# Preparing twelve of a layer's sixteen weight tiles inside the attention stage instead of eight, four of them in place

## The chip, the cores and the metric

The kernel runs on one core of one Trainium2 chip. The metric is the device time of one execution in microseconds (us), given as the median of three runs.

## The reference, cut to what matters

Attention with a computed bias (4 batches, 8 heads, 576 positions, 64 per head), then two feed-forward layers of width 2048 over the 2304 tokens. The weights arrive as 64-bit floats.

```python
scores = scale * np.matmul(q, k.transpose(0, 1, 3, 2)) + bias
attn = np.exp(scores - np.max(scores, axis=-1, keepdims=True))
attn = attn / (np.sum(attn, axis=-1, keepdims=True) + 1e-09)
x = np.matmul(attn, v)                    # 2304 tokens x 512
h = x @ moe_w_in;  x = (h * np.cos(h)) @ moe_w_out
h = x @ moe2_w_in
out = (np.maximum(h, 0.0) + alpha * np.minimum(h, 0.0)) @ moe2_w_out
```

## The kernel before

**Attention.** The eight heads are taken two at a time, so there are 16 pairs (head pair, batch), head pairs outermost. A pair has five row blocks: two in its unit A, three in its unit B (a half-size one first). For each block TensorE computes the scores (L339), VectorE adds the bias and takes the row minimum of the negated sum in one pass out of PSUM (L355), ScalarE takes the exponential (L368). Transposes on TensorE (L421, L386, L430, L443), copies out of PSUM on VectorE and ScalarE (L408, L406) and the products with v (L456, L453) follow as "fillers" between later score blocks. The variable `j` of the loop counts 64 rows; it runs from 0 to 144, nine per pair. Units A of the first four pairs come first, then their units B, then the other twelve pairs one after another, from `j` = 36 on.

**Weight tiles.** Each layer has 16 weight tiles `f`; a tile has two halves, part 0 from `w_in` and part 1 from `w_out`, each 128 x 512. `weight` is a generator that prepares one half: SyncE's queue issues the load of the raw 64-bit words (`raw`, two buffers, L168); ScalarE reads the upper and the lower words (L172 into `c`, L173 into `p`, two buffers each); VectorE moves the exponent and the sign into place (L175, L176); GpSimd adds the low bits (L179). The 32-bit result is split into a rounded high part (L187 on GpSimd, L189 on ScalarE) and the rest (L193, GpSimd or VectorE), because TensorE multiplies high and low parts apart. `HIA` and `LOP` say which engine does the two last steps: GpSimd for halves of layer 0 prepared in attention, ScalarE and VectorE for the others. `stage_w` prepares a half in a tile `st` and stores it to DRAM (`w_d`, L200); `fetch_w` brings a whole tile back by a DMA on GpSimd's queue (L208); `direct_w` prepares a half in the place where the layer uses it.

`bg` is the list of such generators; `step(n)` advances it by n yields. In attention a half of layer 0 is added every `WSR` = 6.5 of `j` from `WS0` = 24 on and one step is made per `j`. Tiles 0 to 7 go this way; 0 to 3 are fetched in the last four blocks of attention, 4 to 7 in the first units of the feed-forward stage. Tiles 8 to 15 are prepared in place while layer 0 works on its first token tile, with `QUOTA0` = 9 steps per unit.

**Feed-forward.** There are five token tiles `t` (three of 512, two of 384) and 16 `f` per layer and tile; one (layer, `t`, `f`) is a unit. A unit's 12 matmuls `h` (L622) run four units (`LA`) ahead of its 12 matmuls `o` (L671, L673). Between them stands the activation of layer 0: L631 (ScalarE), L632 and L633 (VectorE), L635 (ScalarE), L636 (VectorE), then the split L654 (ScalarE) and L655 (GpSimd). After a token tile's last `o`, `evac` copies the four sums out of PSUM (L681, L683), and the next token tile's `o` needs these four banks.

**Order.** Each engine takes its instructions in an order fixed when the program is built. A planner lays them out on a simulated timeline by priority, which is program order apart from `high_priority` blocks; it puts an instruction ahead of earlier ones when its inputs and its buffer are there in that simulation. The two last steps of each weight half are kept in program order (`keep`, `KEEP`).

Of the kernel before, what the change touches and what calls it, by code (L numbers as in the profile page):

```python
# [9 lines left out]
F32 = mybir.dt.float32  # L10
F32R = mybir.dt.float32r
# [22 lines left out]
HIA = (2, 1, 1, 1)  # L34
LOP = (1, 0, 0, 0)
EV_A, EV_M = 5, 6
UPB, EPB = {"D": 11, "A": 4}, 4
PBUF, BTB = 6, 10
FIRST, SIDE, SMOD, BFIRST, BRATE, SPL, WS0, WSR, PER = 4, 6, 2, 16, 1.25, 3, 24, 6.5, 1.0
XL, XS, OEB, LA = 7, 12, 3, 4  # L40
KEEP = (1, 1)
QUOTA0, QUOTA1, NSF = 9, 2, 8
ELAG = 1


# [15 lines left out]
def attn_mlp_kernel(ctx: ExitStack, tc: tile.TileContext, a: dict, out: bass.AP):  # L61
    nc = tc.nc
    ve, se, ge, te, sy = nc.vector, nc.scalar, nc.gpsimd, nc.tensor, nc.sync
# [93 lines left out]
    wt = {}  # L157
    wpool = {}
    keep = lambda k, ins: tc.keep_in_program_order(ins) if k < len(KEEP) and KEEP[k] else ins
    wide = a["wi1"].dtype == I64  # L160
    w_d = [dr.tile([NF, 128, 2, 1024], F32, tag=f"w_d{i}", name=f"w_d{i}") for i in range(2)]

    def weight(layer, f, part, hi, lo, hi_act, lo_pool):
        src = (a["wi1"], a["wi2"])[layer][f] if part == 0 else (a["wo1"], a["wo2"])[layer][f * 128:(f + 1) * 128, :]
        nm = f"{layer}_{f}_{part}"
        if wide:
            raw = wpool["s"].tile([128, 512, 2], I32, tag="raw", name=f"raw{nm}")
            sy.dma_start(out=raw.rearrange("p n t -> p (n t)"), in_=src.bitcast(I32))  # L168
            yield
            c = wpool["c"].tile([128, 512], I32, tag="c", name=f"wc{nm}")  # L170
            p = wpool["c"].tile([128, 512], I32, tag="p", name=f"wp{nm}")
            se.activation(out=c.bitcast(F32), in_=raw[:, :, 1].bitcast(F32), func=AF.Copy, scale=2.0 ** -112)  # L172
            se.activation(out=p, in_=raw[:, :, 0].bitcast(U32), func=AF.Copy, scale=2.0 ** -29)  # L173
            yield
            ve.tensor_scalar(c, c, 3, None, op0=ALU.logical_shift_left)  # L175
            ve.scalar_tensor_tensor(out=c, in0=raw[:, :, 1], scalar=-2 ** 31, in1=c,  # L176
                                    op0=ALU.bitwise_and, op1=ALU.bitwise_or)
            yield
            ge.tensor_tensor(out=c, in0=c, in1=p, op=ALU.add)  # L179
            yield  # L180
            w = c.bitcast(F32)
        else:
            w = wpool["s"].tile([128, 512], F32, tag="raw", name=f"raw{nm}")
            sy.dma_start(out=w, in_=src)
            yield
        if hi_act == 2:
            keep(0, ge.tensor_copy(out=hi, in_=w))  # L187
        elif hi_act:
            keep(0, se.activation(out=hi, in_=w, func=AF.Copy))  # L189
        else:  # L190
            keep(0, ve.tensor_copy(out=hi, in_=w))
        yield
        keep(1, (ge if lo_pool else ve).tensor_tensor(out=lo, in0=w, in1=hi.bitcast(F32), op=ALU.subtract))  # L193
        yield

    def stage_w(layer, f, part):
        t = wpool["c"].tile([128, 2, 512], F32R, tag="st", bufs=1, name=f"st{layer}_{f}_{part}")
        yield from weight(layer, f, part, t[:, 0, :], t[:, 1, :], HIA[layer], LOP[layer])
        yield
        sy.dma_start(out=w_d[layer][f, :, :, 512 * part:512 * part + 512], in_=t.bitcast(F32))  # L200
# [6 lines left out]
    def fetch_w(layer, f):  # L207
        ge.dma_start(out=slot(layer, f), in_=w_d[layer][f])  # L208

    def direct_w(layer, f, part):  # L210
        t = slot(layer, f) if part == 0 else wt[layer, f]
        sl = slice(512 * part, 512 * part + 512)
        yield from weight(layer, f, part, t[:, 0, sl], t[:, 1, sl], HIA[layer + 2], LOP[layer + 2])

    bg = []

    def step(n=1):
        for _ in range(n):
            if not bg:
                return  # L220
            g = bg.pop(0)
            try:
                with tc.high_priority(offset=LP):
                    next(g)
            except StopIteration:
                continue
            bg.insert(min(1, len(bg)), g)
# [9 lines left out]
    def attention():  # L237
        with ExitStack() as c:
# [269 lines left out]
            def more_bias(g):  # L508
                nonlocal ng
                while ng < min(g, NG):  # L510
                    next(bias)
                    ng += 1
                    if ng >= SIDE and ng % SMOD == 0:
                        next(side, None)
                    for s, m in GNEED.items():
                        if ng == m:
                            for h in range(2 if s else 1):
                                load_bias(0, s + 4 * h)
                    if ng == NG:
                        for _ in side:  # L520
                            pass
                        bstack.close()
                        for _ in range(2):
                            ps_t.append(c.enter_context(tc.tile_pool(name="ps_8", bufs=1, space=PSUM, reuse_waits="tile")))
                        right = dict(side="right", reuse_waits="tile")
                        wpool["s"] = ctx.enter_context(tc.tile_pool(name="ws", bufs=2, **right))
                        wpool["c"] = ctx.enter_context(tc.tile_pool(name="wc", bufs=2, **right))
                        wpool["a"] = ctx.enter_context(tc.tile_pool(name="wa", bufs=4, **right))

            pend_exp = []  # L530
            fill = []
            waiting = list(units)
            splits = {}
            credit = 0.0
            ns = 0
            NS = len(stages)
            i = j = 0
            while i < NS or pend_exp or waiting or fill:
                new = []
                if i < NS:  # L540
                    n, u, s = stages[i]
                    hp, b = pairs[n]
                    more_bias(max(BFIRST + int(BRATE * j), GNEED[s]))
                    for m in range(FIRST, NP):
                        f = pos[m, 1]
                        if i == f - 6:
                            load_qkv(m)
                            splits[m] = split_qk(m)
                        if f - SPL <= i < f:
                            next(splits[m], None)  # L550
                    while n not in done:
                        next(side, None)
                    pss = emit_S(n, s)
                    new = [(n, s, h) + emit_max(n, s, h, ps) for h, ps in enumerate(pss)]
                for x in range(len(pend_exp) if i >= NS else len(pend_exp) + len(new) - ELAG):
                    if not pend_exp:
                        pend_exp, new = new, []
                    emit_exp(*pend_exp.pop(0))
                pend_exp += new
                if i < NS:  # L560
                    if b == B - 1 and hp + 1 < NHP:
                        for h in range(len(pss)):
                            load_bias(hp + 1, s + 4 * h)
                    if ng == NG and ns < 2 * NSF and j >= WS0 + WSR * ns:
                        bg.append(stage_w(0, ns // 2, ns % 2))
                        ns += 1
                    if i >= NS - 4:
                        fetch_w(0, i - (NS - 4))
                while waiting and all((waiting[0][0], *k) in Pt for k in place if place[k][0] == waiting[0][1]):
                    recip(*waiting[0])  # L570
                    fill += fillers(*waiting.pop(0))
                m = 2 if s else 1
                credit += PER * m
                while fill and (credit > 0 or i >= NS):
                    d, fn = fill.pop(0)
                    credit -= d
                    fn()
                if not fill:
                    credit = min(credit, 0.0)
                step(m)  # L580
                j += m
                i += 1
            step(100)
# [2 lines left out]
    def mlp():  # L586
        with ExitStack() as c:
            xh_p = c.enter_context(tc.tile_pool(name="xh", bufs=8, reuse_waits="tile"))
            g_p = c.enter_context(tc.tile_pool(name="gp", bufs=3, reuse_waits="tile"))
            t_p = c.enter_context(tc.tile_pool(name="tp", bufs=2, reuse_waits="tile"))  # L590
            wpool["b"] = c.enter_context(tc.tile_pool(name="wb", bufs=12, reuse_waits="tile"))
            ph = c.enter_context(tc.tile_pool(name="ph", bufs=4, space=PSUM, reuse_waits="tile"))
            po = c.enter_context(tc.tile_pool(name="po", bufs=4, space=PSUM, reuse_waits="tile"))
# [2 lines left out]
            raw = {}  # L596
# [103 lines left out]
            for j in range(len(units) + LA):  # L700
                quota = 0
                if j < len(units):
                    L, t, f = units[j]
# [8 lines left out]
                    if L == 0 and t == NTI - 1 and f >= 6 and f % 2 == 0 or L == 1 and t == 0 and 2 <= f < 5:  # L712
                        fetch_w(1, nf)
                        nf += 1
                    quota = QUOTA0 if t == 0 else QUOTA1
                    ps = emit_h(L, t, f)
                    acts.append((act1 if L == 0 else act2)(t, f, ps))
                    next(acts[-1])
# [20 lines left out]

    attention()  # L740
    mlp()


# [60 lines left out]
```

## Time and profile before

| | |
|---|---|
| median of three runs | 1181.04 us (1180.21 to 1185.94) |
| the profiled execution, its own time | 1182.64 us |
| its span, first to last instruction | 1180.9 us |
| mean granted TensorE clock | 0.981 |
| TensorE matmul busy | 1127.7 us (96%) |
| VectorE, ScalarE, GpSimd busy | 696.4, 517.2, 437.1 us |

Busy matmul time is not the engine at its peak, since ends of matmuls are modelled. Attention lasts to about 361 us of the span, the feed-forward stage from there. "[2.00 <-DMA raw]" behind an instruction means that its engine stood idle 2.00 us before it, until that event. The engines are called PE (TensorE), PEld (its weight loads), DVE (VectorE), ACT (ScalarE), POOL (GpSimd) and SP (SyncE).

### The profile page before, as it was taken

The numbers are of one execution on the slowest core, as the hardware profiler recorded it, in microseconds if no ns is written. First come the engines' busy times: TensorE is split into PE (matmuls) and PEld (weight loads), VectorE is DVE, ScalarE is ACT, GpSimd is POOL, SyncE is SP. The second block draws the span as 40 slices with busy tenths as digits, with TensorE's granted clock in tenths as the row PEclk, the third lists the DMA queues.
The fourth block names the chain that finished last, engine by engine and source line by source line (L and its number), as shares of the span: only waits on it lengthen the run. The fifth ranks groups of instructions, "written<-read, shape, count | busy, mean of one in ns | idle before, by whom it ended". The sixth has DMA issues, their size and how long they took to land.

```text
span 1180.9 us, 17191 instructions
## 1 busy us (share of the span) xinstructions
PE 1127.7 (96%) x6376; PEld 891.5 (75%) x6376; DVE 696.4 (59%) x1278; ACT 517.2 (44%) x1006; POOL 437.1 (37%) x400
## 2 busy tenths in 40 slices
PE   5698998999998999899999999999999999999998
PEld 1245665666665887788888999988888888889997
DVE  8796566666667987555555556696742332332322
ACT  5586666665665764444443544434411111111111
POOL 5104445445314654333333334454632222322222
PEclk9699999999999999899999999999999999999999
DMA  7657546746316532212212325553310000000000
GB/s 244 199 145 251 186 150 205 235 156 204 104 58 211 206 124 91 78 66 63 90 54 63 108 90 173 192 193 120 106 37 1 27 37 1 27 36 1 27 1 27
DMA packets 56083, 129.47 MB, mean 110 GB/s; under 512 B 8000, under 2 KB 15168, under 8 KB 53952
## 3 DMA queue, kind: packets, MB, share of 16 engines
q1 hardware_dynamic: 53696, 111.60, 29.2%
q0 software_dynamic: 2304, 16.78, 4.1%
q8 instruction: 50, 0.82, 0.3%
q14 instruction: 33, 0.27, 0.1%
HBM read 86.53 MB, written 41.83 MB: 109 GB/s over the span
## 4 chain that ended last, share of the span: by engine, by line
PE 77%; DVE 9%; DMA 5%; ACT 5%; issue 3%; POOL 0%; SPq 0%; DVEq 0%; ACTq 0%; POOLq 0%
PE h L622 29%; PE o L673 17%; PE o L671 14%; PE S L339 5%; PE x_B L456 3%; DVE u L122 2%; PE T_A L421 2%; PE T_B L421 2%; DMA raw<-in_wi_dram 1%; PE x_A L456 1%; DMA raw<-in_wo_dram 1%; PE bps L127 1%; DVE P L355 1%; DMA bias_d<-be 1%; ACT P L368 1%
## 5 line engine op out<-in xcount | busy, mean ns | idle before, releaser
L622 PE MATMUL h<-xhi,w 128*128 128x512 f32 (+1 forms) x1280 | 394.3, 370 | 0.6 <-DVE w L193 0.6
L655 POOL TENSOR_TENSOR glo<-tb,ghi 128x512 fp32r<-128x512 f32 (+1 forms) x160 | 197.4, 1234 | 427.3 <-ACT ghi L654 390.3
L622 PEld LDWEIGHTS h<-xhi,w 128*128 128x128 f32 x1280 | 237.9, 188 | 34.3 <-DVE w L193 1.0
L622 PE MATMUL h<-xlo,w 128*128 128x512 f32 (+1 forms) x640 | 236.5, 370 | 0.0
L654 ACT ACTIVATE ghi<-tb 128x512 fp32r<-128x512 f32 (+1 forms) x160 | 93.1, 583 | 284.2 <-PE o L673 248.7
L671 PE MATMUL o<-ghi,w 128*128 128x512 f32 (+1 forms) x640 | 199.5, 372 | 4.5 <-ACT oe L681 3.4
L673 PE MATMUL o<-w,ghi 128*128 128x512 f32 x576 | 192.1, 392 | 0.0
L644 DVE TENSOR_SCALAR tb<-h,alpha 128x512 f32<-128x512 f32 (+1 forms) x80 | 55.6, 695 | 199.2 <-PE h L622 189.8
L671 PEld LDWEIGHTS o<-ghi,w 128*128 128x128 f32 x640 | 119.7, 189 | 21.4 <-ACT oe L681 3.8
L622 PEld LDWEIGHTS h<-xlo,w 128*128 128x128 f32 x640 | 120.3, 188 | 17.7 <-issue 0.5
L673 PEld LDWEIGHTS o<-w,ghi 128*128 128x128 f32 x576 | 108.2, 188 | 22.7
L179 POOL TENSOR_TENSOR wc<-wc,wp 128x512 int32<-128x512 int32 x64 | 87.7, 1370 | 97.8 <-DVE wc L176 77.8
L671 PE MATMUL o<-glo,w 128*128 128x512 f32 (+1 forms) x320 | 118.7, 371 | 0.7 <-POOL glo L655 0.7
L368 ACT ACTIVATE P<-P,nm 128x576 f32<-128x576 f32 x128 | 98.3, 771 | 45.2 <-DVE nm L355 45.1
L673 PE MATMUL o<-w,glo 128*128 128x512 f32 x288 | 112.9, 392 | 0.0
L355 DVE CUSTOM_DVE_ANT_0 P<-S,bt 128x576 f32<-128x576 f32 x128 | 91.8, 753 | 26.8 <-PE S L339 25.3
L635 ACT ACTIVATE tb<-tb,hpi 128x512 f32<-128x512 f32 (+1 forms) x80 | 54.3, 679 | 101.5 <-DVE tb L633 101.4
L632 DVE SCALAR_TENSOR_TENSOR tb<-ta,h 128x512 f32<-128x512 int32 (+1 forms) x80 | 50.3, 629 | 60.2 <-ACT ta L631 40.2
L636 DVE TENSOR_TENSOR tb<-h,tb 128x512 f32<-128x512 f32 (+1 forms) x80 | 50.8, 635 | 53.8 <-ACT tb L635 53.7
L173 ACT ACTIVATE wp<-raw 128x512 int32<-128x512 uint32 x64 | 42.9, 670 | 62.0 <-DMA raw<-in_wo_dram 32.0
L671 PEld LDWEIGHTS o<-glo,w 128*128 128x128 f32 x320 | 60.7, 190 | 9.1 <-POOL glo L655 1.1
L339 PE MATMUL S<-kh,qh 64*128 64x288 f32 (+1 forms) x288 | 56.7, 349 | 9.2 <-DVE nm L355 9.2
(100 smaller groups left out, 1603.5 us busy)
## 6 DMA issues: line engine op xcount, KB each, us to landing
raw<-in_wi_dram SPq DMA_DIRECT2D x32, 512.0 KB, 3.5
raw<-in_wo_dram SPq DMA_DIRECT2D x32, 512.0 KB, 3.5
w_d<-st SPq DMA_DIRECT2D x32, 512.0 KB, 3.1
w<-w_d POOLq DMA_DIRECT2D x16, 1024.0 KB, 6.7
bias_d<-be SPq DMA_DIRECT2D x36, 295.5 KB, 3.3
xlo<-x_d SPq DMA_DIRECT2D x24, 256.0 KB, 4.3
rq<-in_q_dram SPq DMA_DIRECT2D x16, 320.0 KB, 3.2
rk<-in_k_dram SPq DMA_DIRECT2D x16, 320.0 KB, 3.5
```

What stands on the lines that cost most here:

```text
L179: ge.tensor_tensor(out=c, in0=c, in1=p, op=ALU.add)
L339: te.matmul(ps[:, hf, 0:HS], lhsT=w[r, 128 * i:128 * i + 128], rhs=m[r, c0:c0 + HS], start=(j == 0), stop=(j == 2))
L355: keep(2, ve.tensor_tensor_reduce(out=sn.rearrange("p (a b) -> p a b", a=2), in0=ps[:, :, 0:HS], in1=bt[hp, s].rearrange("p (a b) -> p a b ...
L368: keep(3, se.activation(out=e, in_=e, func=AF.Exp, bias=nm, scale=-1.0, accum_out=sums[n, u][:, col, 0:1]))
L622: te.matmul(ps[:, 0:n], lhsT=w_[:, wx, w], rhs=xx[:, 0:n], start=(j == 0), stop=(j == 11))
L635: se.activation(out=g, in_=g, func=AF.Sin, bias=hpi)
L636: ve.tensor_tensor(out=g, in0=h, in1=g, op=ALU.mult)
L644: ve.tensor_scalar(g, h, 0.0, alpha[:, f:f + 1], op0=ALU.min, op1=ALU.mult)
L654: se.activation(out=ghi[:, 0:n], in_=g, func=AF.Copy)
L655: ge.tensor_tensor(out=glo[:, 0:n], in0=g, in1=ghi[:, 0:n].bitcast(F32), op=ALU.subtract)
L671: te.matmul(acc[L, t][i][:, 0:n], lhsT=w_[:, wx, wl], rhs=gx[:, 0:n], start=st, stop=sp)
L673: te.matmul(acc[L, t][i], lhsT=gx[:, sl], rhs=w_[:, wx, 512:1024], start=st, stop=sp)
```

## The change

Layer 0's halves are added in attention from `j` = 22 on, every 4.6 of `j`, and 1.5 steps are made per `j`. Tiles 0 to 3 (halves 0 to 7) are prepared in place by `direct_w`, with GpSimd for the last two steps as in `stage_w`; tiles 4 to 11 are staged through DRAM as before and fetched in the first eight units of the feed-forward stage. The four fetches at attention's end are gone. Tiles 12 to 15 are left for the first token tile, with 6 steps per unit (layer 1 keeps 9). The load of a half's raw words is written one half ahead of its generator, and `st` has two buffers in attention.

```diff
-FIRST, SIDE, SMOD, BFIRST, BRATE, SPL, WS0, WSR, PER = 4, 6, 2, 16, 1.25, 3, 24, 6.5, 1.0
+FIRST, SIDE, SMOD, BFIRST, BRATE, SPL, WS0, WSR, PER = 4, 6, 2, 16, 1.25, 3, 22, 4.6, 1.0
+SR = 1.5
-QUOTA0, QUOTA1, NSF = 9, 2, 8
+QUOTA0, QUOTA1, NSF = (6, 9), 2, 12
...
+    raws_w = {}
+
+    def load_raw(layer, f, part):
...
+            raw = wpool["s"].tile([128, 512, 2], I32, tag="raw", name=f"raw{nm}")
+            sy.dma_start(out=raw.rearrange("p n t -> p (n t)"), in_=src.bitcast(I32))
...
+        raws_w[layer, f, part] = raw
...
     def weight(layer, f, part, hi, lo, hi_act, lo_pool):
...
-            raw = wpool["s"].tile([128, 512, 2], I32, tag="raw", name=f"raw{nm}")
-            sy.dma_start(out=raw.rearrange("p n t -> p (n t)"), in_=src.bitcast(I32))
-            yield
+            if (layer, f, part) not in raws_w:
+                load_raw(layer, f, part)
+                yield
+            raw = raws_w.pop((layer, f, part))
...
     def stage_w(layer, f, part):
-        t = wpool["c"].tile([128, 2, 512], F32R, tag="st", bufs=1, name=f"st{layer}_{f}_{part}")
+        t = wpool["t"].tile([128, 2, 512], F32R, tag="st", name=f"st{layer}_{f}_{part}")
...
-    def direct_w(layer, f, part):
+    def direct_w(layer, f, part, ahead=0):
...
-        yield from weight(layer, f, part, t[:, 0, sl], t[:, 1, sl], HIA[layer + 2], LOP[layer + 2])
+        i = layer + 2 - 2 * ahead
+        yield from weight(layer, f, part, t[:, 0, sl], t[:, 1, sl], HIA[i], LOP[i])
...
+                        wpool["t"] = c.enter_context(tc.tile_pool(name="wt", bufs=2, **right))
...
                     if ng == NG and ns < 2 * NSF and j >= WS0 + WSR * ns:
-                        bg.append(stage_w(0, ns // 2, ns % 2))
+                        if ns == 0:
+                            load_raw(0, 0, 0)
+                        if ns + 1 < 2 * NSF:
+                            load_raw(0, (ns + 1) // 2, (ns + 1) % 2)
+                        bg.append(direct_w(0, ns // 2, ns % 2, 1) if ns < 8 else stage_w(0, ns // 2, ns % 2))
                         ns += 1
-                    if i >= NS - 4:
-                        fetch_w(0, i - (NS - 4))
...
-                step(m)
+                wsteps += SR * m
+                step(int(wsteps))
+                wsteps -= int(wsteps)
...
+            wpool["t"] = c.enter_context(tc.tile_pool(name="wt", bufs=1, reuse_waits="tile"))
...
-                    quota = QUOTA0 if t == 0 else QUOTA1
+                    quota = QUOTA0[L] if t == 0 else QUOTA1
```

## Rows read from the trace of the kernel before

**Rows 1.** The page's first line.

```profile
span 1180.9 us, 17191 instructions
```

**Rows 2.** Busy time by stretch: PE, PEld, DVE, ACT, POOL, clock, DMA share, GB/s.

```profile
100.00:361.00 261.00, 247.58 (x1997) 166.98 (x1994) 172.88 (x447) 166.66 (x381) 110.89 (x122) 0.99 0.51 165
390.00:450.00 60.00, 59.44 (x261) 48.65 (x260) 56.41 (x73) 42.55 (x72) 36.45 (x26) 1.00 0.44 142
480.80:486.60 5.80, 5.72 (x14) 4.50 (x15) 4.52 (x7) 2.96 (x6) 2.96 (x2) 0.50 0.99 320
```

**Rows 3.** Busy time, weight preparation (tile wc) on VectorE alone, first token tile.

```profile
390.00:450.00 60.00, 35.59 (x41) 1.00 0.44 142
```

**Rows 4.** The same view, the activation (tile tb) on VectorE alone.

```profile
390.00:450.00 60.00, 23.87 (x32) 1.00 0.44 142
```

**Rows 5.** The chain that ended last, one undisturbed unit: start, duration, what.

```profile
502.70 2.73 PE h L622 x12
505.43 2.72 PE o L671 x12
```

**Rows 6.** Timeline to the end of the first token tile: start, duration, instruction.

```profile
445.80 0.72 PE L622 MATMUL h<-xhi,w 128*128 128x512 f32 x2 [0.56 <-DVE w L193]
...
454.86 0.50 PE L671 MATMUL o<-glo,w 128*128 128x512 f32 x1 [0.71 <-POOL glo L655]
...
477.59 1.39 DVE L193 TENSOR_TENSOR st<-wc,st 128x512 fp32r<-128x512 f32 x1 [0.35 <-ACT st L189]
...
479.71 0.43 DVE L175 TENSOR_SCALAR wc<-wc 128x512 int32<-128x512 int32 x1 [0.73 <-ACT wc L172]
480.05 0.68 DVE L683 COPY oe<-o 128x512 f32<-128x512 f32 x1
...
480.88 0.76 PE L671 MATMUL o<-ghi,w 128*128 128x512 f32 x1 [3.44 <-ACT oe L681]
```

**Rows 7.** Groups of instructions in attention, 100 to 361 us, weight preparation only.

```profile
L179 POOL TENSOR_TENSOR wc<-wc,wp 128x512 int32<-128x512 int32 x16 | 20.5, 1278 | 39.2 <-DVE wc L176 19.9 <-DVE sm_A L377 9.6 <-ACT wp L173 5.1
L193 POOL TENSOR_TENSOR st<-wc,st 128x512 fp32r<-128x512 f32 x15 | 19.1, 1276 | 0.2
...
L176 DVE SCALAR_TENSOR_TENSOR wc<-raw,wc 128x512 int32<-128x512 int32 x17 | 12.5, 737 | 0.3
L173 ACT ACTIVATE wp<-raw 128x512 int32<-128x512 uint32 x18 | 12.1, 674 | 14.0 <-DMA raw<-in_wo_dram 7.9 <-DMA raw<-in_wi_dram 3.6 <-POOL ql L326 2.4
L172 ACT ACTIVATE wc<-raw 128x512 f32<-128x512 f32 x17 | 11.2, 661 | 0.8 <-DMA bias_d<-be 0.8
L187 POOL CAST st<-wc 128x512 fp32r<-128x512 f32 x16 | 10.4, 648 | 19.6 <-DMA w_d<-st 19.6
L175 DVE TENSOR_SCALAR wc<-wc 128x512 int32<-128x512 int32 x17 | 7.8, 460 | 11.4 <-ACT wc L172 11.4
```

**Rows 8.** Eleven pairs from first score to first score, with ACT L173 alone.

```profile
193.61:215.48 21.87, 1.31 (x2) 0.92 0.75 236
...
269.64:290.28 20.64, 1.34 (x2) 0.92 0.73 226
...
sum 203.98, ACT 8.06; mean ACT 0.73
```

**Rows 9.** The same eleven pairs, with DVE L176 alone.

```profile
215.48:233.93 18.45, 1.37 (x2) 1.00 0.68 230
...
307.80:326.09 18.29, 1.59 (x2) 1.00 0.38 131
```

**Rows 10.** Timeline inside the first pair of rows 8.

```profile
195.57 0.66 ACT L173 ACTIVATE wp<-raw 128x512 int32<-128x512 uint32 x1 [2.00 <-DMA raw<-in_wo_dram]
...
197.31 0.34 PE L386 MATMUL T_B<-ident,Pr 128*64 128x64 f32 x4 [1.40 <-ACT T_B L406]
...
199.37 0.40 PE L339 MATMUL S<-kh,qh 64*128 64x288 f32 x2 [1.36 <-DVE nm L355]
```

**Rows 11.** The page's DMA issues: KB each, median us to landing.

```profile
w<-w_d POOLq DMA_DIRECT2D x16, 1024.0 KB, 6.7
```

More of the change, by code (lines that the diff above doesn't have):

```diff
@@ L161, in attn_mlp_kernel @@
     w_d = [dr.tile([NF, 128, 2, 1024], F32, tag=f"w_d{i}", name=f"w_d{i}") for i in range(2)]
-    def weight(layer, f, part, hi, lo, hi_act, lo_pool):
+    raws_w = {}
+    def load_raw(layer, f, part):
         src = (a["wi1"], a["wi2"])[layer][f] if part == 0 else (a["wo1"], a["wo2"])[layer][f * 128:(f + 1) * 128, :]
@@ L168, in weight @@
             sy.dma_start(out=raw.rearrange("p n t -> p (n t)"), in_=src.bitcast(I32))
-            yield
+        else:
+            raw = wpool["s"].tile([128, 512], F32, tag="raw", name=f"raw{nm}")
+            sy.dma_start(out=raw, in_=src)
+        raws_w[layer, f, part] = raw
+    def weight(layer, f, part, hi, lo, hi_act, lo_pool):
+        nm = f"{layer}_{f}_{part}"
+        if wide:
+            if (layer, f, part) not in raws_w:
+                load_raw(layer, f, part)
+                yield
+            raw = raws_w.pop((layer, f, part))
             c = wpool["c"].tile([128, 512], I32, tag="c", name=f"wc{nm}")
@@ L182, in weight @@
         else:
-            w = wpool["s"].tile([128, 512], F32, tag="raw", name=f"raw{nm}")
-            sy.dma_start(out=w, in_=src)
-            yield
+            if (layer, f, part) not in raws_w:
+                load_raw(layer, f, part)
+                yield
+            w = raws_w.pop((layer, f, part))
         if hi_act == 2:
@@ L534, in attention @@
             credit = 0.0
+            wsteps = 0.0
             ns = 0
```

## Prediction

> **What bounds the kernel now.** I read the page first, then the busy time by stretch, then the timeline wherever a stretch lost matmuls, then the groups of instructions in attention and the busy time pair by pair. The profiled execution took 1182.64 us, of which 1180.9 lie in the span [rows 1] and 1.7 around it; it is 1.6 above the median of 1181.04. The sum below is made against 1182.64, and what it changes is then taken from the median.
>
> In the feed-forward stage TensorE sets the pace: an undisturbed unit, twelve h and twelve o, takes 2.73 + 2.72 = 5.45 us [rows 5], and no other engine matters as long as it keeps up. The stretch where one does not keep up is layer 0's first token tile. From 390 to 450 us VectorE is busy 56.4 of 60 us [rows 2]. Of that work the weight preparation takes 35.59 us in 41 instructions, three to a half, so 2.60 us per half [rows 3], and the activation 23.87 us in 32, three to a unit, so 2.24 us per unit [rows 4]. (The two overlap a little at their seams, so they add to more than the union.) The reader can check the overload: 9 steps per unit at 7 yields per half are 1.29 halves, and 1.29 x 2.60 + 2.24 = 5.6 us of VectorE in a unit of 5.45. In these 60 us VectorE finished 32 / 3 = 10.7 units' activation where TensorE could do 60 / 5.45 = 11. TensorE hides the lag behind its lead of four units until that is used up. Then it stands 0.56 us for a late weight and 0.71 us for a late activation, and at the end of the token tile 3.44 us for the evacuation [rows 6]: VectorE took the evacuating copy L683 only at 480.05, behind L193 and L175 of layer 1's weights. The clock fell after that stall and was granted at 0.50 (1.2 of 2.4 GHz) for 5.80 us [rows 2], which is worth half of it, 2.9 us.
>
> In attention TensorE shows 247.6 busy us of 261, while VectorE (172.9), ScalarE (166.7) and GpSimd (110.9) have room [rows 2]. Eleven pairs that run one after another take 203.98 us. Two of them stick out, 21.87 and 20.64 us [rows 8]; the other nine average (203.98 - 21.87 - 20.64) / 9 = 17.94. These two are the only ones in which L173, which reads raw words, runs twice. Inside the first, ScalarE stood 2.00 us at the head of its queue for the raw load; the copies and exponentials behind it were late, TensorE stood 1.40 and 1.36 us [rows 10], and the pair's clock mean is 0.92 [rows 8].
>
> **The change part by part.**
>
> *Eight halves leave the first token tile.* VectorE loses 8 x 2.60 = 20.8 us there. The density falls to 6 / 7 = 0.86 halves per unit, so 0.86 x 2.60 + 2.24 = 4.5 us per 5.45: from 103% to 82%, below capacity with 1 us per unit to spare. The lag no longer builds up, and with it go the two small stalls (0.56 + 0.71), the evacuation stall (3.44) and the slow clock behind it (2.9): 7.6 us together. The layer-1 instructions ahead of the evacuation keep their program place, so I bound this from below by the first two alone: 1.3 us.
>
> *Eight halves are added to attention.* One costs ScalarE 661 + 674 ns, VectorE 460 + 737 ns and GpSimd 1278 + 648 + 1276 ns [rows 7]; eight cost 10.7, 9.6 and 25.6 us. All three engines have that room [rows 2], so busy time is not the price; the price is that each instruction stands in order ahead of a score's minimum, an exponential or a copy. Low bound: nothing, since the nine other pairs lie near 17.94 whether they read no raw load or one. High bound: the two held pairs as the price of a second half, (21.87 + 20.64) / 2 - 17.94 = 3.3 us each, x 8 = 26.5. In between lie the two pairs that did the VectorE pass L176 twice without a late load: 18.45 and 18.29 [rows 9], 0.43 above 17.94. I take that row, since it holds the added VectorE work without the accident of a late load: 8 x 0.43 = 3.4 us.
>
> *The steps* must fit: 8 halves x 6 yields + 16 x 7 = 160, and 1.5 x (144 - 22) = 183 are offered, so attention ends with nothing owed. Before, 128 were owed against 120.
>
> *In place and two `st` buffers.* GpSimd's 19.6 us of waiting for the store of `st` [rows 7] should shrink. GpSimd waits on other engines anyway, so I count 0.
>
> *The fetches.* The stores stay sixteen. Four fetches leave attention, and the first token tile has eight instead of four. Each lands 6.7 us after its issue [rows 11]; it is written at unit i for unit i + 4, that is 4 x 5.45 = 21.8 us ahead, so I count 0. Its cover gone, it is a rival below.
>
> *The load half a tile ahead.* With two `raw` buffers a load can go only when the half before the previous one has been read. If the planner already puts loads at that point, writing the load earlier moves nothing; I take 0, with the removal of the held pairs as the other end, -6.6 (3.9 + 2.7).
>
> *Sum:* -7.6 + 3.4 = -4.2 us, 1178.4 for the profiled execution's own time, 1176.8 against the median.
>
> *A rule against the change.* At the stretch of [rows 3] a VectorE preparation instruction averages 35.59 / 41 = 868 ns; in attention the two it has there average (460 + 737) / 2 = 598 [rows 7]. The Trainium skill, page "SBUF — State Buffer", section "Who interferes with whom", says that a VectorE instruction with two SBUF inputs and a GpSimd instruction that reads SBUF shut each other out for a whole instruction; the change puts all its new GpSimd work beside attention's VectorE. By that rule the sum would gain a term (the port rival below); by the 598 ns, measured with sixteen halves beside GpSimd, it does not.
>
> **The rivals.**
>
> *Held pairs (slower).* After the change a half comes every 4.6 of `j` and a pair is nine, so nearly every pair converts two raw loads, and so far both pairs that did were held at 3.3 us. At H held pairs attention changes by 3.3 x (H - 2). It eats the 7.6 from H = 4.3 on and is slower by over 0.5% from six on; with seven, +16.5 - 7.6 = +8.9, 1190. For it: two out of two. Against: pairs next to them had as much VectorE work at 18.4, and the loads were late there, not the work itself.
>
> *Loads early enough.* The load half a tile ahead does remove the held pairs: -4.2 - 6.6 = -10.8, 1170.2. For it: the only large losses in attention start at a raw load. Against: the two buffers.
>
> *The evacuation stall stays,* since layer 1's kept instructions still stand ahead of L683: only 1.3 is won, +2.1, 1183.1.
>
> *Late fetches.* If the eight go strictly one after another, each is 6.7 - 5.45 = 1.25 us later than its unit needs, so up to 10 us late at the eighth: +5.8, 1186.8. Against: four units of lead, and DMA engines that are 0.44 busy in that stretch [rows 2].
>
> *Port.* If GpSimd's new work lengthens the preparation in attention to 868 ns as in [rows 3], 24 halves x 2 x 0.27 = 13 us of VectorE stand ahead of score minima: +8.8 if all is on the path, 1189.8.
>
> **How the numbers follow.** A measurement of this kernel tells about 0.5%, 5.9 us, from no change: 1175.1 to 1186.9. The forecast as summed has 0.42 and its own range is 1173 to 1180 (3.4 between 0 and 7), of which 0.13 falls below 1175.1. Loads early enough 0.21, held pairs 0.16, the stall stays 0.11, late fetches 0.06, port 0.04. Faster: 0.21 + 0.13 = 0.34. Slower: 0.13 of the held pairs (six or more), 0.03 each of the last two: 0.19. Within: 0.47. The range must hold the forecast, the stalls that stay, most of the early loads and some held pairs: 1167 to 1188.
>
> **What would show it.** Right: between 390 and 477 us VectorE at about 80%, no TensorE stall at the end of the first token tile and no clock of 0.50 there, and 24 fewer VectorE preparation instructions in the first token tile (8 x 3). Attention's steps: pairs with two L173 at 18 to 18.5 us (my sum), at 21 (held pairs), or no pair above 18.5 (early loads). SyncE's raw loads still issued as soon as a buffer comes free would show that writing them earlier moved nothing. Wrong: a TensorE wait for a tile fetched by L208, an evacuation copy still behind L193, or attention longer by more than 7.6 us.

## The result and the profile after

The changed kernel takes 1171.3 us (median of 4 runs, 1168.49 to 1173.1), the kernel before 1181.03 beside it (4 runs): a ratio of 0.9915, 95% interval 0.9894 to 0.9936, 0.85% faster. The profiled execution took 1172.02 us with a span of 1170.3. Against the span of before [rows 1] that is 10.6 us less.

The busy time of the changed kernel by stretch has the columns of [rows 2]. The first stretch is attention; the next two are most of layer 0's first token tile, and the last is its end.

```profile
100.00:361.00 261.00, 246.77 (x1999) 167.76 (x1997) 193.79 (x469) 178.19 (x402) 138.12 (x145) 0.99 0.54 173
390.00:450.00 60.00, 60.00 (x265) 49.48 (x264) 43.26 (x57) 32.49 (x54) 28.36 (x24) 1.00 0.51 185
450.00:477.00 27.00, 27.00 (x119) 22.07 (x118) 17.72 (x24) 13.18 (x21) 9.67 (x8) 1.00 0.24 79
477.00:487.00 10.00, 10.00 (x44) 8.10 (x44) 4.14 (x6) 4.07 (x7) 2.54 (x3) 1.00 0.00 0
```

TensorE is busy without a hole through the whole first token tile, where it stood 3.44 us before [rows 6], and the clock stays at 1.00 where 5.80 us ran at 0.50 [rows 2]. VectorE went from 56.41 [rows 2] to 43.26 of 60 us. Its two kinds of work in the same stretch, in the view of [rows 3, 4], first the weight preparation, then the activation:

```profile
390.00:450.00 60.00, 14.65 (x18) 1.00 0.51 185
390.00:450.00 60.00, 27.52 (x35) 1.00 0.51 185
```

There are 23 fewer preparation instructions, and 35 of the activation for 32: VectorE now keeps pace with TensorE's eleven units. The timeline of the changed kernel at the end of the token tile shows VectorE's evacuating copy without an idle time or a queue before it (columns as in [rows 6]):

```profile
467.60 0.43 DVE L190 TENSOR_SCALAR wc<-wc 128x512 int32<-128x512 int32 x1 [0.73 <-ACT wc L187]
467.94 0.68 DVE L707 COPY oe<-o 128x512 f32<-128x512 f32 x1
```

A layer-1 instruction still stands just ahead of it, but VectorE is no longer behind.

The span can be cut at four instructions that the timeline shows: the first score of the fifth pair, the first score of the last pair, the last pair's last score block, and the first h.

| stretch, us | before | after | difference |
|---|---|---|---|
| start to the fifth pair | 140.6 | 144.0 | +3.4 |
| eleven pairs | 204.0 | 202.0 | -2.0 |
| last pair, to its last score block | 15.6 | 13.1 | -2.5 |
| from there to the first h | 7.3 | 5.5 | -1.8 |
| feed-forward, to the end | 813.4 | 805.7 | -7.7 |

The feed-forward stage gained what was forecast for it. Attention gained too, where 3.4 us of loss had been forecast.

### The profile page after: what moved, and what is told of

It reads as the page before. It is cut to its first block, busy times and chain, and to the rows that moved or that the text cites. A ratio compares the mean times of both kernels' runs of the same rounds, so it can differ in the third digit from the quotient of the medians.

```text
span 1170.3 us, 17227 instructions
## 1 busy us (share of the span) xinstructions
PE 1121.2 (96%) x6376; PEld 891.2 (76%) x6376; DVE 694.6 (59%) x1270; ACT 513.1 (44%) x998; POOL 451.8 (39%) x416
## 4 chain that ended last, share of the span: by engine, by line
PE 71%; DVE 10%; DMA 8%; ACT 5%; issue 4%; POOL 2%; SPq 0%; DVEq 0%; ACTq 0%; POOLq 0%
PE h L646 28%; PE o L697 15%; PE o L695 13%; PE S L356 4%; DMA raw<-in_wo_dram 4%; PE x_B L473 3%; DVE u L123 3%; PE T_A L438 2%; DMA raw<-in_wi_dram 2%; DVE P L372 1%; DVE wc L191 1%; PE T_B L438 1%; PE x_A L473 1%; PE bps L128 1%; ACT P L385 1%
## 5 line engine op out<-in xcount | busy, mean ns | idle before, releaser
L372 DVE CUSTOM_DVE_ANT_0 P<-S,bt 128x576 f32<-128x576 f32 x128 | 91.7, 753 | 25.3 <-PE S L356 22.3
L188 ACT ACTIVATE wp<-raw 128x512 int32<-128x512 uint32 x64 | 43.0, 672 | 57.8 <-DMA raw<-in_wi_dram 28.9
```

Source lines behind the costliest of these rows:

```text
L372: keep(2, ve.tensor_tensor_reduce(out=sn.rearrange("p (a b) -> p a b", a=2), in0=ps[:, :, 0:HS], in1=bt[hp, s].rearrange("p (a b) -> p a b ...
```

## The experiments

Each kernel was timed against the kernel before on its own chip and profiled once. In the table, a held pair is one of the eleven that takes over 20 us; "long" counts VectorE's preparation instructions (L190 and L191, or the lines that answer to them) of over 0.9 us in the eleven pairs; "end" is the last pair and the stretch to the first h together.

| kernel | median us | ratio, 95% interval | eleven pairs | held | long | end | feed-forward |
|---|---|---|---|---|---|---|---|
| before | 1181.03 | 1 | 204.0 | 2 | 1 | 22.9 | 813.4 |
| after | 1171.3 | 0.9915 [0.9894, 0.9936] | 202.0 | 1 | 10 | 18.6 | 805.7 |
| e13 (after again) | 1170.84 | 0.9896 [0.9863, 0.993] | 199.9 | 1 | 11 | 18.5 | 806.0 |
| e1 | 1168.77 | 0.9881 [0.9854, 0.9908] | 203.8 | 0 | 8 | 18.5 | 806.9 |
| e2 | 1176.86 | 0.9942 [0.9921, 0.9962] | 201.7 | 1 | 11 | 18.6 | 813.5 |
| e3 | 1181.2 | 0.9988 [0.9969, 1.0006] | 209.5 | 4 | 5 | 18.5 | 811.9 |
| e5 | 1173.2 | 0.9918 [0.9891, 0.9945] | 201.4 | 0 | 11 | 18.5 | 805.4 |
| e6 | 1175.17 | 0.9937 [0.9914, 0.9961] | 193.5 | 0 | 2 | 23.0 | 815.6 |
| e7 | 1176.96 | 0.9944 [0.9918, 0.9971] | 209.1 | 3 | 7 | 18.5 | 805.6 |
| e8 | 1179.41 | 0.9974 [0.995, 0.9999] | 199.2 | 1 | 5 | 25.4 | 814.1 |
| e9 | 1173.67 | 0.9914 [0.9885, 0.9943] | 204.9 | 1 | 11 | 19.2 | 805.0 |
| e10 | 1169.37 | 0.9883 [0.9851, 0.9916] | 199.7 | 1 | 9 | 18.5 | 807.5 |
| e11 | 1177.35 | 0.995 [0.9929, 0.9971] | 199.4 | 1 | 6 | 19.4 | 814.5 |
| e12 | 1176.59 | 0.9952 [0.9932, 0.9973] | 195.5 | 0 | 1 | 22.9 | 812.3 |

The two profiles of the changed kernel differ by 2.1 us in the eleven pairs and by 2.5 in the span (1170.3 and 1167.7), so a difference of that size between two single profiles says nothing. The stretches are those of the one profiled execution, which can lie well above its kernel's median (by 4.2 us in e8, 3.9 in e2, 3.5 in e1, 2.9 in e7), so they do not add up to differences of medians.

**e1: the raw load not ahead.** The changed kernel without the early loads; 1.75 steps per `j` pay for the yield that comes back.

```diff
-SR = 1.5
+SR = 1.75
...
-                        if ns == 0:
-                            load_raw(0, 0, 0)
-                        if ns + 1 < 2 * NSF:
-                            load_raw(0, (ns + 1) // 2, (ns + 1) % 2)
```

> The changed kernel with one part undone: each half asks for its own raw words as its first step, and 1.75 steps per 64 rows make up for that extra step, so each half is done at the same row as in the changed kernel. Theory (the planner already issues a raw load when its buffer comes free, so writing it earlier moves nothing): 1171 within 4 us, pairs with two raw loads still near 17.6 us, raw loads issued as before at the moment a buffer is released. Rival (the load half a tile ahead is what keeps ScalarE from standing for raw words): several pairs held at 20.5 to 22 us, 1177 to 1185.

0.9881, not slower than the changed kernel, with 203.8 us in the eleven pairs. The early load is worth nothing that shows. The queue's own waits in the changed kernel's trace, 144 to 346 us, where it issues 20 raw loads, fit that (line, what it waited for, total us, times, longest):

```profile
SPq L172 <- DVE wc L191: 44.8, 19, 5.0
```

19 of the 20 waited until VectorE had read a buffer, so a load written earlier goes no earlier.

**e2: the preparation work put back.** The changed kernel, with eight halves prepared once more in layer 0's first token tile at nine steps per unit; their result goes to a spare tile that nothing reads.

```diff
-QUOTA0, QUOTA1, NSF = (6, 9), 2, 12
+QUOTA0, QUOTA1, NSF = (9, 9), 2, 12
...
+    def again_w(f, part):
+        t = wpool["t"].tile([128, 2, 512], F32R, tag="st", name=f"again{f}_{part}")
+        yield from weight(0, f, part, t[:, 0, :], t[:, 1, :], HIA[2], LOP[2])
...
+                        if L == 0:
+                            bg.extend(again_w(8 + i // 2, i % 2) for i in range(8))
```

> The changed kernel with eight halves (tiles 8 to 11) prepared a second time in layer 0's first token tile, into a scratch tile that nothing reads, ahead of the eight real ones and at 9 steps per unit: the preparation work of the kernel before is back in that stretch, and nothing else is. Theory (7.6 us of the gain come from VectorE's load there): first matmul h as in the changed kernel near 364.5 us, VectorE over 90% busy from 390 to 450 us, the stall at the end of the token tile and a clock of 0.50 behind it are back, 1177 to 1180. Rival (the gain in the feed-forward stage comes from the order at the token tile's end or from the fetches): no stall at the end of the token tile, 1171 to 1173.

The feed-forward stage takes 813.5 us, 7.8 more than the changed kernel and within 0.2 of the kernel before. TensorE's timeline shows the late weights again:

```profile
436.90 0.50 PE L650 MATMUL h<-xhi,w 128*128 128x512 f32 x1 [0.55 <-ACT w L205]
445.12 0.51 PE L650 MATMUL h<-xhi,w 128*128 128x512 f32 x1 [1.30 <-ACT w L205]
446.97 0.72 PE L650 MATMUL h<-xhi,w 128*128 128x512 f32 x2 [0.64 <-DVE w L209]
```

A wait of 1.56 us for the evacuation follows at 478.7. Two of the signs expected are missing: VectorE is busy 82% from 390 to 450 us, not over 90%, and the clock behind the wait is 1.00, not 0.50.

```profile
390.00:450.00 60.00, 57.51 (x250) 46.28 (x249) 49.06 (x64) 39.45 (x66) 31.29 (x23) 1.00 0.55 201
```

So the preparation work, put back alone, costs as much of this stage as the change had won, but more of it by late weights and less by the evacuation than in the kernel before. It runs on ScalarE too (L205), so VectorE's share is not told apart. The profiled execution was the slowest of e2's eight; by the ratios, 0.9942 to 0.9915 and 0.9896, the whole kernel loses 3 to 5 us, less than this one profile shows.

**e3: the kernel before, its halves finished earlier.** Eight tiles as before, a half every 5.5 of `j` and 1.5 steps per `j`, so that nothing is owed in the last pair.

```diff
-FIRST, SIDE, SMOD, BFIRST, BRATE, SPL, WS0, WSR, PER = 4, 6, 2, 16, 1.25, 3, 24, 6.5, 1.0
+FIRST, SIDE, SMOD, BFIRST, BRATE, SPL, WS0, WSR, PER = 4, 6, 2, 16, 1.25, 3, 24, 5.5, 1.0
+SR = 1.5
...
-                step(m)
+                wsteps += SR * m
+                step(int(wsteps))
+                wsteps -= int(wsteps)
```

> The kernel before with only the pace of its sixteen halves in attention changed: every 5.5 instead of 6.5 of the row count and 1.5 steps per 64 rows, so that the last one ends a quarter of attention earlier; eight tiles staged and eight prepared in the first token tile as before. Theory (a last pair free of weight work gives 4.4 us: 2.5 in the pair, 1.8 in the passage to the feed-forward stage): 1176 to 1178, the first h about 4 us after less time from the last pair's first score, the stall near the end of the first token tile still there. Rival (the last pair is short for some other reason, such as the fetches being gone): 1180 to 1182. If fewer halves at the end were all, the last pair would hold no weight instruction and take 13 us.

The end goes from 22.9 to 18.5 us, the whole gain of the changed kernel there (13.1 + 5.4), but four held pairs make the eleven 5.5 longer, and the time is that of before. In the first held pair ScalarE stands for a raw load:

```profile
174.40 0.66 ACT L174 ACTIVATE wp<-raw 128x512 int32<-128x512 uint32 x1 [4.94 <-DMA raw<-in_wo_dram]
```

That load was issued at 166.8 us and landed after 7.5; at 166.1 GpSimd had issued one of the four whole-tile fetches that the program writes at attention's end:

```profile
166.12 0.57 POOL L209 DMA_DIRECT2D w<-w_d  x1
```

In the next held pair a fetch runs too; in the other two, from 254.1 and from 312.2 us on, none does.

**e6 and e12: four tiles in place, without and with the stores.** e6 is the kernel before with tiles 0 to 3 prepared by `direct_w` and without their stores and fetches. e12 is e6 with their eight stores put back; nothing reads them.

```diff
...
-                        bg.append(stage_w(0, ns // 2, ns % 2))
+                        bg.append(direct_w(0, ns // 2, ns % 2, 1) if ns < 8 else stage_w(0, ns // 2, ns % 2))
                         ns += 1
-                    if i >= NS - 4:
-                        fetch_w(0, i - (NS - 4))
```

> The kernel before with one thing changed in attention: its first four tiles (halves 0 to 7) are prepared in place and the four fetches in attention are gone; pace, number of halves, one st buffer and the first token tile are as before. Theory (a 1 MB fetch beside a raw load makes the load late, ScalarE stands for it and the pair is held; without fetches no pair is): pairs all under 19 us, attention 4 to 7 us shorter, the stall at the end of the first token tile still there, 1175 to 1179 beside a kernel before of 1183. Rival (late raw loads come from the v, x and st transfers as well, so the fetches are not the cause): one or two pairs over 20 us, 1181 to 1184.

e12 adds, in `direct_w`:

```diff
+        if ahead:
+            yield
+            sy.dma_start(out=w_d[layer][f, :, :, sl], in_=t[:, :, sl].bitcast(F32))
```

> The kernel before with tiles 0 to 3 prepared in place and without their four fetches, as in the earlier run, but with the eight stores of these halves to w_d kept (nothing reads them): the stores and the fetches told apart. Theory A (the fetches on GpSimd's queue beside the raw loads hold the pairs): the eleven pairs stay near 193.5, none above 18.5, no raw landing above 5 us, about 0.994 of the kernel before. Theory B (the stores on SyncE's queue, between the raw loads, hold them): pairs above 20 us come back, eleven pairs 200 to 204, about the time of the kernel before.

In e6 no pair of the eleven is held. The sum and the longest pair of the view of [rows 8]:

```profile
298.73:317.03 18.30, 0.67 (x1) 1.00 0.22 75
...
sum 193.52, ACT 8.25; mean ACT 0.75
```

204.0 became 193.5, -10.5 us, and the raw loads of that stretch land in 3.3 to 4.6 us. With the stores it is 195.5 with the longest pair 18.47, and the ratios of the two, 0.9937 and 0.9952, lie in one another's intervals. So the stores cost little or nothing, and with the four tiles in place and no fetch no pair is held. That the fetches alone held the pairs is not shown, since no run takes out nothing else: tiles in place need no `st` either, and GpSimd's wait for its store, 19.6 us from 100 to 361 us before [rows 7], is 13.3 in e6 and 12.5 in e12. Here is e6's (total us, times, longest):

```profile
POOL st L187 <- DMA w_d<-st: 13.3, 4, 3.6
```

One raw load of e12 did land in 5.4 us, with no fetch beside it.

**e7: the fetches put back into the changed kernel.** All twelve tiles staged through DRAM, tiles 0 to 3 fetched as before.

```diff
-                        bg.append(direct_w(0, ns // 2, ns % 2, 1) if ns < 8 else stage_w(0, ns // 2, ns % 2))
+                        bg.append(stage_w(0, ns // 2, ns % 2))
...
+                    if i >= NS - 4:
+                        fetch_w(0, i - (NS - 4))
```

> The changed kernel with tiles 0 to 3 staged through DRAM and fetched in attention as in the kernel before, all else as changed (24 halves, pace, load ahead, two st buffers, 6 steps per unit). Theory (the fetches hold pairs): two to four more pairs over 20 us, attention 5 to 9 us longer, 1177 to 1182; the feed-forward stage from the first h as in the changed kernel, 805.7 us. Rival (the load ahead or the two st buffers keep ScalarE from standing): 1171 to 1174, no more held pairs than the one at 323 us.

Three held pairs and 209.1 us, 7 more than the changed kernel and 9 more than e13; by the ratios, 0.9944 to 0.9915 and 0.9896, the whole kernel loses 3 to 6 us. The edit puts the staging of the four tiles back with their fetches. In the first held pair ScalarE waits for the raw load issued at 183.9, 0.7 us behind a fetch. The view of its tile says:

```profile
  ACT wp L188: 3.7, 1
...
DMA to landing us min/median/max: 8.1/8.1/8.1
```

In the other two held pairs, from 221.7 and from 332.8 us on, no fetch runs; the second of them is the eleventh pair, the one held in the changed kernel too.

**e8: the kernel before with two `st` buffers.**

```diff
-        t = wpool["c"].tile([128, 2, 512], F32R, tag="st", bufs=1, name=f"st{layer}_{f}_{part}")
+        t = wpool["t"].tile([128, 2, 512], F32R, tag="st", name=f"st{layer}_{f}_{part}")
...
+                        wpool["t"] = c.enter_context(tc.tile_pool(name="wt", bufs=2, **right))
...
```

> The kernel before with two st buffers in attention instead of one and nothing else changed. Theory (GpSimd's 19.6 us of waiting for the store of st lies beside other waits): GpSimd's wait for the store gone, 1181 to 1184 beside a kernel before of 1183, both held pairs still there. Rival (a late GpSimd releases the buffers late, so raw loads are issued late and ScalarE stands): pairs all under 19 us, 1176 to 1179.

0.9974: at most a small gain. One held pair is left of two; the start (143.1) and the stretch to the first h (9.8) grew. By this one profile the eleven pairs are 4.8 us shorter with all four fetches still there, so part of what e6 and e12 show may be the wait for `st`.

**e5 and e9: the halves later, and more of them.** e5 starts the halves ten `j` later (`WS0` 32, nothing else); e9 prepares fourteen tiles in attention:

```diff
-FIRST, SIDE, SMOD, BFIRST, BRATE, SPL, WS0, WSR, PER = 4, 6, 2, 16, 1.25, 3, 22, 4.6, 1.0
+FIRST, SIDE, SMOD, BFIRST, BRATE, SPL, WS0, WSR, PER = 4, 6, 2, 16, 1.25, 3, 20, 4.0, 1.0
-SR = 1.5
+SR = 1.75
...
-QUOTA0, QUOTA1, NSF = (6, 9), 2, 12
+QUOTA0, QUOTA1, NSF = (4, 9), 2, 14
```

> The changed kernel with its 24 halves started ten counts of 64 rows later (32 instead of 22), so that they run into the last pair. Theory (the gain of 3 us in attention sits in a last pair free of weight work): last pair back to about 15.6 us and the passage to the first h back to 7 us, 1174 to 1177. Rival (it comes from the pairs before): 1170 to 1172.

> The changed kernel taken on: fourteen tiles in attention instead of twelve, every 4.0 of the row count from 20 on, 1.75 steps per 64 rows, 4 steps per unit in the first token tile. Theory (the first token tile has no stall left to win back, and attention still has room for two raw loads per pair): feed-forward stage still near 805.7 us, attention 0 to 4 us longer, 1170 to 1176. Rival (a price per half in attention of 0.4 us or more appears only now): over 1176; or further gain in the feed-forward stage: under 1168.

e5 shifted little: only one L188 falls into the last pair, which still takes 13.06 us, so it says nothing on what weight work costs there. e9 gains nothing over twelve tiles: 204.9 us in the eleven pairs for 0.7 us less of feed-forward.

**e10, e11, e13: ten tiles, nine tiles, and the changed kernel beside them.**

```diff
-FIRST, SIDE, SMOD, BFIRST, BRATE, SPL, WS0, WSR, PER = 4, 6, 2, 16, 1.25, 3, 22, 4.6, 1.0
+FIRST, SIDE, SMOD, BFIRST, BRATE, SPL, WS0, WSR, PER = 4, 6, 2, 16, 1.25, 3, 22, 5.5, 1.0
-SR = 1.5
+SR = 1.375
...
-QUOTA0, QUOTA1, NSF = (6, 9), 2, 12
+QUOTA0, QUOTA1, NSF = (6, 9), 2, 10
```

e11 has 6.1, 1.25, (7, 9) and 9 in these places: seven tiles are left to the first token tile.

> The changed kernel with ten instead of twelve tiles in attention (a half every 5.5 of j, 1.375 steps per j; the other six tiles are left to the first token tile, six steps per unit as before). Theory (each half in attention costs about 1.06 us, since eight more cost 202.0 - 193.5 = 8.5; the first token tile stays below VectorE's capacity at 6/7 halves per unit however many tiles are left, as long as it ends in time): attention's eleven pairs 197.7 us, four less than with twelve tiles; feed-forward stage unchanged at 805.7; about 0.35% faster than the changed kernel, about 0.9878 of the kernel before. Rival 1 (the held pairs, not the halves, set attention's length): one or two pairs above 20 us remain and the eleven pairs stay at 201 to 204, total as the changed kernel's. Rival 2 (more weight work in the first token tile): stalls of VectorE's evacuation come back, feed-forward 808 or more.

> The changed kernel with nine tiles in attention (a half every 6.1 of j, 1.25 steps per j) and seven tiles in the first token tile at seven steps per unit. Theory: eleven pairs 195.6 us (193.5 with eight tiles in place and no fetches, plus two halves at 1.06); VectorE in the first token tile 1.0 half per unit x 2.60 + 2.24 = 4.84 of 5.45 us, so no stall at its end and 805.7 for the stage; about 0.985 of the kernel before, the fastest of all. Rival: at 89% VectorE's lag does build up, or the last tiles are late, and the stall of 3 to 4 us with its slow clock comes back: feed-forward 809 to 814 and the total at or above the changed kernel's.

> The changed kernel once more, on the same chip as the kernels with ten and with nine tiles, to be compared with them there: about 0.9915 of the kernel before; eleven pairs about 202, feed-forward stage about 805.7.

The price of 1.06 us per half fell as a rule: 199.7 and 199.4 us where it gave 197.7 and 195.6. Ten tiles are not told apart from twelve (0.9883 and 0.9896). Nine are slower, and the trace of e11 names the place. TensorE waits there not for the evacuation but for a weight:

```profile
444.13 1.14 ACT L205 ACTIVATE w<-wc 128x512 fp32r<-128x512 f32 x2
...
444.80 0.80 PE L646 MATMUL h<-xhi,w 128*128 128x512 f32 x1 [5.43 <-ACT w L205]
```

That h belongs to the token tile's sixteenth unit, whose weight is the last of the seven: it comes too late, and the granted clock averages 0.71 over the 11.6 us from 439.4 on. The sum for e11, 1.0 x 2.60 + 2.24 = 4.84 of 5.45 us, said that VectorE would keep up on average; it did not say that the last tile would be in time.

## Why the prediction was right, and where it was not

The time, 1171.3, lies in the range, 5.5 us below the forecast of 1176.8; it lies outside 0.5%, while the likeliest of the three outcomes was within it. In the profile the sum was -4.2 and the span shows -10.6. That the range holds the time is in part luck: the prediction gave its own sum 1173 to 1180, the wider range stood for rivals that did not come, and two terms that it had at nothing outweighed one that it had too small. Step by step:

**Eight halves leave the first token tile: right.** -7.6 was forecast, -7.7 measured, and e2 brings 7.8 back, though by another mix of waits. Matmul by matmul, the changed kernel gains 1.9 us where the two small stalls were and 6.3 at the evacuation with its slow clock, and loses 0.5 again in the second layer. Each sign named is there: no stall at the end, no 0.50, 23 fewer preparation instructions for the 24 of the whole tile. VectorE is at 43.26 / 60 = 72%, not 80: the stretch held 18 / 3 = 6 halves in 11 units, not 0.86 per unit. The rival in which the evacuation stall stays falls with that.

**"Four fetches leave attention ... so I count 0": the step that failed,** together with the 0 for the tiles in place. The prediction costed only the fetches' landing in the feed-forward stage and never what they did where they were, since the program writes them in the last four blocks. The view of their tile in the trace of before shows where they ran (count, ns, first and last issue):

```profile
L208 POOL DMA_DIRECT2D w<-w_d x4: 567/568/697, 151.9 to 243.9; - x4
...
DMA to landing us min/median/max: 5.5/5.7/6.8
```

The planner had put each soon after its tile was stored, in the middle of attention. The second went at 187.36; the raw load behind which the first held pair [rows 8, 10] stood was issued at 189.73 and landed after 5.8 us, where the one issued alone at 165.3 took 3.4:

```profile
187.36 0.57 POOL L208 DMA_DIRECT2D w<-w_d  x1
```

```profile
189.73 0.33 SPq L168 DMA_DIRECT2D raw<-in_wo_dram  x1
```

The four tiles in place without their fetches are worth 10.5 us of the eleven pairs in e6 and 8.5 in e12; the way back costs 7 in e7. How much of that is the fetches' own stays open. The Trainium skill, page "DMA: Bandwidth & Descriptors", section "Issuing engines are not separate DMA queues", says that transfers started by different engines end on the same 16 DMA engines and interleave there. The landings of 5.8, 7.5 and 8.1 us beside a fetch agree.

A fetch is not the only cause of a held pair. Of the ten in before, e3, e7 and e8, five had no fetch running in them nor beside a raw load that they waited for; ahead of the second of before [rows 8] the load issued at 265.4 took 5.4 us without one. Loads are late beside other transfers too: with no fetch in attention the slowest in the eleven pairs took 6.6 us in the changed kernel, and in e9, in the view of `raw`:

```profile
DMA to landing us min/median/max: 3.5/3.8/7.6
```

Nor does a late load always hold a pair. In the kernel before ScalarE stood 2.45 us for one at 253.40, behind the fourth fetch, and that pair took 18.1 us.

**"Eight halves are added to attention", 3.4 us: right in sign, mis-sized.** From e6, which has the same four tiles in place and no fetches, to the changed kernel the eleven pairs grow from 193.5 to 202.0, or 199.9 in e13: 6.4 to 8.5 us. It is no price per half: e11, with two halves more than e6, already has 5.9 of it, and the pace, the early load and the second `st` differ as well. What TensorE waited for most in the eleven pairs, in e6 and in the changed kernel, is the row minimum (total us, times, longest):

```profile
PE S L340 <- DVE nm L356: 3.9, 10, 0.5
PE S L356 <- DVE nm L372: 7.8, 10, 1.9
```

The rows taken for the price had seen little of what the denser work brings on. The groups of [rows 7], in the changed kernel:

```profile
L191 DVE SCALAR_TENSOR_TENSOR wc<-raw,wc 128x512 int32<-128x512 int32 x26 | 23.1, 891 | 0.5
...
L190 DVE TENSOR_SCALAR wc<-wc 128x512 int32<-128x512 int32 x26 | 19.0, 730 | 4.2 <-ACT wc L187 4.2
```

460 and 737 ns became 730 and 891, with medians still at 425 and 692. So a few became long: 13 of the 52 took 0.94 to 1.91 us, and each began while a GpSimd instruction ran and ended after it. The rule has no exception here: 19 of the 52 began while a GpSimd instruction ran, and every one ended 0.28 or 0.29 us (L190) or 0.54 or 0.55 us (L191) after that instruction; of the other 33 none took over 0.70 us. Three of the long ones, from the timeline:

```profile
267.23 1.31 POOL L194 TENSOR_TENSOR wc<-wc,wp 128x512 int32<-128x512 int32 x1 [1.55 <-DVE wc L191]
...
267.43 1.66 DVE L191 SCALAR_TENSOR_TENSOR wc<-raw,wc 128x512 int32<-128x512 int32 x1
...
271.19 0.40 PE L356 MATMUL S<-kh,qh 64*128 64x288 f32 x2 [1.54 <-DVE nm L372]
...
283.72 1.55 POOL L343 TENSOR_TENSOR ql<-rq,qh 128x640 fp32r<-128x640 f32 x1
283.84 1.71 DVE L190 TENSOR_SCALAR wc<-wc 128x512 int32<-128x512 int32 x1
...
326.59 1.44 POOL L209 TENSOR_TENSOR st<-wc,st 128x512 fp32r<-128x512 f32 x1
...
326.94 1.64 DVE L191 SCALAR_TENSOR_TENSOR wc<-raw,wc 128x512 int32<-128x512 int32 x1
...
328.50 0.74 DVE L372 CUSTOM_DVE_ANT_0 P<-S,bt 128x576 f32<-128x576 f32 x1
...
329.98 0.61 PE L356 MATMUL S<-kh,qh 64*128 64x288 f32 x2 [1.85 <-DVE nm L372]
```

The last lines are the one held pair of the changed kernel, 22.49 us: L191 ends 0.5 us after L209, the row minimum L372 starts behind it, and TensorE stands 1.85 us. ScalarE had waited 1.17 us for a raw load just before, so both shares are in that pair. TensorE's three longest waits for a row minimum in the eleven pairs (1.85, 1.54 and, at 308.87, 0.92 us) all stand behind such a long L191. The extra against the medians is 26 x (730 - 425 + 891 - 692) = 13.1 us of VectorE in 100 to 361 us. Reckoned as the port rival did, mean against mean of before, it is 26 x (730 - 460 + 891 - 737) = 11.0, near that rival's 13, which had 0.04. It was not all on the path, as the rival's +8.8 had it: the waits for the row minimum grew by 3.9 us. The Trainium skill, page "SBUF — State Buffer", section "Who interferes with whom", has this: a VectorE instruction with two SBUF inputs and a GpSimd instruction that reads SBUF, or a `tensor_scalar` in a two-port mode and GpSimd, exclude each other for a whole instruction. The trace agrees for L191, which has two SBUF inputs; L190 has one and is held in the same way, and no row tells the mode that it ran in. What is shown is the lengthening, and three of TensorE's waits behind it. That it makes up the rest of the longer pairs is argued from the table (2 and 1 long ones at 193.5 and 195.5 us, 6 to 11 at 199 to 205 without fetches), and no run changed GpSimd's share alone.

**What was counted nowhere: the end of attention, -4.3.** "Attention ends with nothing owed" was in the prediction, with no price. Without weight work the last pair takes 13.1 us for 15.6 and the stretch to the first h 5.5 for 7.3; GpSimd is busy 0.85 us there:

```profile
346.02:359.09 13.07, 12.68 (x110) 9.31 (x110) 9.19 (x24) 8.21 (x20) 0.85 (x2) 1.00 0.03 11
```

e3 shows the same gain in the kernel before. Why weight work costs time there no run tells apart.

**The start of the span, +3.4, stays open.** 140.6 before, 144.0 and 143.3 after, and 141 to 145 over all the kernels; e8 has 143.1 by its two `st` buffers alone. The planner lays the whole program out anew with every edit, and no run tells such a shift from a cost.

**Two zeros held.** The early load (e1) and the eight fetches in the first token tile: issued at 381.9 to 401.3, their landing took up to 13.6 us (6.7 in [rows 11]), and no matmul waited for one.

**The rivals.** Held pairs by count fell: nine of the changed kernel's eleven pairs run L188 two or three times, and one of the nine takes over 20 us. (At six held pairs that rival's own sum gives 3.3 x 4 - 7.6 = 5.6 us, still inside 0.5%.) Early loads came nearest in time (1170.2), but by a mechanism that e1 refutes.

## What to carry to other kernels

Before a removed transfer is priced at nothing, look up in the trace when it ran, not where the program writes it; and take it out alone before its price is called known. Work moved beside an engine that shares a resource is priced by the tail of the durations, not by an instruction's median: here a quarter of them took 1.5 to 4 times their median. A share of capacity says whether an engine keeps up on average; the deadline of the last piece has to be worked out beside it.

## What was not expected of the hardware

A 512 KB raw load landed in 3.3 to 4.6 us in e6, where no fetch ran, and in 5.8, 7.5 and 8.1 us where a 1 MB fetch had been issued 2.4, 0.7 and 0.7 us ahead of it; but it took up to 7.6 us in e9 with no fetch either. A 128x512 `tensor_scalar` of 425 ns took 1.71 us when it began 0.12 us after a GpSimd instruction of 1.55: it ended 0.28 us after it, as all such did. And one program laid out once differs by 2.5 us of span between two profiled executions, most of it in attention.
